# A second level of the fast product for 40 instead of 18 products of a fused attention and feed-forward kernel, with a new order of its instructions

## The chip, the cores and the metric

One Trainium2 chip, one of its cores. The metric is device time in microseconds (us) of one execution; three runs of the kernel before took 904.32, 905.68 and 908.74, median 905.68. Engines: TensorE (PE in the profile, PEld for its weight loads), VectorE (DVE), ScalarE (ACT), GpSimd (POOL), and SyncE (SP), which here only issues DMAs.

## The reference

Attention over keys and values that are averaged in groups of 8 rows, and a feed-forward layer on its output:

```python
batch, n_heads, seq, head_dim = (8, 8, 576, 64)
k_p = k.reshape(B, H, Sp, pool, D).mean(axis=3)      # pool = 8, Sp = 72
v_p = v.reshape(B, H, Sp, pool, D).mean(axis=3)
scores = scale * np.matmul(q, k_p.transpose(0, 1, 3, 2))
scores = scores - np.max(scores, axis=-1, keepdims=True)
attn = np.exp(scores)
attn = attn / (np.sum(attn, axis=-1, keepdims=True) + 1e-09)
o = np.matmul(attn, v_p).astype(np.float32)
x = np.ascontiguousarray(o.transpose(0, 2, 1, 3)).reshape(B * S, H * D)   # 4608 x 512
h = x @ w_in                                          # 512 x 2048
s = np.sin(alpha * h)
g = h + s * s / (alpha + 1e-09)
return (g @ w_out).astype(np.float32)                 # 2048 x 512
```

All in float32.

## The kernel before

*Units and groups.* The 4608 tokens are cut into nine units of 512 (u = 0 to 8); the first layer's 2048 columns into four groups (J = 0 to 3), so that one group makes a block of 512 tokens by 2 x 2 x 128 columns. Each group is multiplied by the Winograd form of Strassen's scheme: tokens, contraction and columns are each halved, and seven products M1 to M7 replace eight. The sums of weight blocks are made once (`combine_w_in`, L671), those of the activations once per unit (`sums_of_x`, L796, four sums on VectorE into the tile `home3`, called `bt`). A product is four matmuls of 128x128 weights by 256 tokens (L834), added in place in PSUM: M1 is copied to where M6 is added (L810), that sum to where M7 is added, M5 is copied to SBUF (`p5`); M2, M3 and M4 complete the four quarters, with sums on VectorE (L809).

*The second level.* For units 1 to 6 some products are themselves done by seven products of half size (`inner_product`, L1002): M5 in groups 2 and 3, M1 in group 3, three per unit and 18 in all. Each is seven matmuls of 128 columns (L1014) in four steps: `a` (two products into a scratch bank, copied by ScalarE at L1018 and L1020), `b` (two, then the copy of L1024), `d` (one, then VectorE's sum of L1029) and `e` (two). Its weights are made once on GpSimd (`inner_w_in`, L769), its eight sums of activations once per unit (`inner_x`, L782, GpSimd, L794), at slot 2 of the unit that uses them.

*After the products,* for each of the four quarters: ScalarE takes the sine (L984) and the scaled square (L991), VectorE adds (L1036), and the block `h` goes to DRAM (`store_g`, L1047). There are two `h` buffers, and one tile `s` for all sines.

*Attention, alongside.* During unit u, batch u + 1's attention is worked in: `two_scores` (L294, matmuls of L308), maxima and differences on VectorE (L331, L332), exponentials on ScalarE (L357, with a table load before and after), sums and reciprocals on VectorE (L363, L364), scaling on GpSimd (L365), 32x32 turns on VectorE (L491 and after), and 16 DMAs that move the turned weights into `aM` (`move`, L504). `all_values` (L590; matmuls of L600 and L613) multiplies by the values, and `to_x` (L513) copies the result out of PSUM into the next activations (L527). `turn_q` (L206) turns a later batch's queries; `k_t` transposes pooled keys, and L270 copies them. Loads of q, k and v and their pooling on GpSimd (L127) come in between.

*What sets the order.* The order on each engine is the order in which the program issues instructions. `hidden` (L806) goes through 28 slots per unit, seven per group: in each it issues group work, and at one fixed place (`extras`) the attention's pieces, which `carry` (L1154) has entered under slot numbers. PSUM has eight banks: five rotate among the groups' four accumulators and attention (`bank`, L747), and banks 5 to 7 serve scores, values and the second level. After the nine units, the second layer (`outputs`, L1262) runs the same scheme twice over, as matmuls of 128x144 (L1312).

Of the kernel before, what the change touches and what calls it, by code (L numbers as in the profile page):

```python
# [36 lines left out]

class Kernel:
# [91 lines left out]
    def load_v(self, b):  # L133
# [13 lines left out]
        self.pool_rows(t, vm[:])  # L147
# [58 lines left out]
    def turn_q(self, b, part):  # L206
# [5 lines left out]
        if part == 0:  # L212
            self.tr = self.new_tr()
        tr = self.tr[:, 0:2560].rearrange("p (k x) -> p k x", k=2)
        if part == 0:
            for e in range(2):
                x = main[:, 4 * e:4 * e + 4].rearrange("p hp t (k i) -> p hp t k i", i=32).rearrange("p hp t k i -> p (hp t) k i")
                out = tr[:, :, 768 * e:768 * e + 512].rearrange("p k (n i) -> p n k i", i=32)
                nc.vector.transpose(out=out, in_=x)
                if e == 0:  # L220
                    self.finish_before()
            return
# [15 lines left out]

    def new_tr(self):
        return self.ap.tile([P, 20 * 5 * 32], F32, name="tr")[:]  # L240
# [8 lines left out]
    def attention(self, b):  # L249
# [14 lines left out]
        def k_t():  # L264
            kp = self.kp.pop(b)
            m = Sp // 3
            ps = self.abank([P, 3, NP * m])
            for j in range(3):
                nc.tensor.transpose(ps[:, j, :], kp[:, j].rearrange("p e d -> p (e d)"), self.ident[:NP * m, :NP * m])
            nc.vector.tensor_copy(out=kb[:].rearrange("p hp (x j) -> p j hp x", j=3), in_=ps.rearrange("p j (hp x) -> p j hp x", hp=NP))  # L270
# [23 lines left out]
        def two_scores(j):  # L294

            x = (self.turn + 1) % 5
# [14 lines left out]
            two_shifts()  # L311
            if j == 0:
                two_shifts()
# [53 lines left out]
        def new_a():  # L367
            self.aM = self.ap.tile([P, 4, 736], F32, name="aM")
# [86 lines left out]
        def a0_views():  # L455

            x = self.aM[:].rearrange("p a x -> p (a x)")[:, 0:5 * S].rearrange("p (h n) -> p h n", h=5)
            return x[:, 0:4], x[:, 4]
# [26 lines left out]
        def turn(i):  # L485
            if i == 0:
                self.tr = self.new_tr()
# [16 lines left out]
        def move(blocks, queue=nc.sync, halves=(0, 1)):  # L504

            tr = self.tr[:, 0:2944].rearrange("p (c s x) -> p c s x", c=2, s=2)
            for a in blocks:
                for s in halves:
                    for c in range(2):
                        r, w = 64 * s + 32 * c, 704 if c else 736  # L510
                        queue.dma_start(out=self.aM[r:r + 32, a, 0:w], in_=tr[32 * a:32 * a + 32, c, s, 0:w])
# [18 lines left out]
        def value_parts(hp, rest):  # L530
# [9 lines left out]
            if rest:  # L540
                r = 64 * s
                at = lambda r, n, i: self.aM[r:r + n, 2 * g:2 * g + 2, 640 + 32 * i:672 + 32 * i]
# [3 lines left out]
            at = lambda r, n, h: order(self.aM[r:r + n, :, 128 * h:128 * h + 128])  # L546
# [3 lines left out]
        def values(hps, banks, n, d):  # L550
# [8 lines left out]
            if d == 0:  # L559
                self.bt[0] = self.home(3, [P, 4, 2, TH])  # L560
            turned = [o.rearrange("p (t j) -> p j t", t=4) for o in ps]

            def differences():
                for kk, o in enumerate(turned):
                    y = self.bt[0][:, 0, kk] if d else self.xT[0][:, kk, 0:TH]
                    f = lambda x: x.rearrange("p (j t) -> p j t", t=4)
                    nc.vector.scalar_tensor_tensor(out=f(self.bt[0][:, d, kk]), in0=o[:, TH // 4:TH // 2, :], scalar=1.0 / POOL, in1=f(y),
# [22 lines left out]
        def all_values():  # L590

            hps = 0, 2, 1, 3
            ps = dict(zip(hps, (self.psum([P, 4 * P], i) for i in (5, 6, 7, (self.turn + 4) % 5))))
            rest = self.psum([P, 4, 64], (self.turn + 1) % 5)
# [20 lines left out]
            self.behind_order()  # L615
            self.behind_order = lambda: None
            for hp in hps:
                to_x(ps[hp].rearrange("p (t j) -> p j t", t=4), hp, 0, 512)
            to_x(rest, slice(0, 4), 512, 64)

        return SimpleNamespace(**{f.__name__: f for f in (k_t, q_t, products, score, two_scores, two_shifts, exp, norm, new_a, turn, move, values, values_rest, all_values,
# [125 lines left out]
    def bank(self, shape, i=None):  # L747

        if i is None:
            i = self.turn = (self.turn + 1) % 5  # L750
        return self.psum(shape, i)
# [17 lines left out]
    def inner_w_in(self):  # L769

        w = self.q_tile(0)[:]
        at = 0
        for p, J0 in ((5, 2), (1, 3)):
            n = self.NJ - J0
            A = self.A[p][:].rearrange("p k (J j m) -> p k J j m", j=2, m=P)[:, :, J0:]
            L = lambda i, j: A[:, j, :, i]
            s1, s2, s3, s4 = (w[:, at + i * n * P:at + (i + 1) * n * P].rearrange("p (J m) -> p J m", m=P) for i in range(4))
            at += 4 * n * P
            self.sums(((s1, L(1, 0), L(1, 1), OP.add), (s2, s1, L(0, 0), OP.subtract), (s3, L(0, 0), L(1, 0), OP.subtract), (s4, L(0, 1), s2, OP.subtract)))
            self.W2[p] = J0, {1: L(0, 0), 2: L(0, 1), 3: s4, 4: L(1, 1), 5: s1, 6: s2, 7: s3}  # L780

    def inner_x(self, u):  # L782

        for p, x, out in ((5, self.bt[u][:, 0], self.last[:, 0:4 * P]),
                          (1, self.xT[u][:, 0:2, 0:TH], self.ex[:, 5].rearrange("p h x -> p (h x)")[:, 0:4 * P])):
            R = lambda i, j: x[:, i, j * P:(j + 1) * P]
            t1, t2, t3, t4 = (out[:, i * P:(i + 1) * P] for i in range(4))
            self.sums(((t1, R(0, 1), R(0, 0), OP.subtract), (t2, R(1, 1), t1, OP.subtract), (t3, R(1, 1), R(0, 1), OP.subtract), (t4, R(1, 0), t2, OP.subtract)))
            self.X2[p] = {1: R(0, 0), 2: R(1, 0), 3: R(1, 1), 4: t4, 5: t1, 6: t2, 7: t3}

# [5 lines left out]
    def sums_of_x(self, u, n):  # L796

        nc = self.nc
        if u not in self.bt:
            self.bt[u] = self.home(3, [P, 4, 2, TH])  # L800
        xT, bt = self.xT[u], self.bt[u]
# [4 lines left out]
    def hidden(self, u, extra):  # L806

        nc = self.nc
        add = lambda o, x, y: nc.vector.tensor_tensor(out=o, in0=x, in1=y, op=OP.add)  # L809
        copy = lambda o, x: nc.scalar.copy(out=o, in_=x)  # L810
        sin, square, early = self.sin, self.square, lambda G: G.J == (0 if G.u else 1)
        two = 0 < u < self.B - 1

        def begin(J):

            b1, b6, b5, b7 = (self.bank([P, JW, TH]) for _ in range(4))
            new = lambda n, **kw: self.hp.tile([P, 2, JW, 2, TH], F32, name=n, **kw)
            G = SimpleNamespace(u=u, J=J, b1=b1, b5=b5, b6=b6, b7=b7, g=new("h"), s=self.s,
                                p5=None, i1=None, i5=None, early=J == (0 if u else 1))
            if two and J > 1:  # L820
                G.i5 = self.inner_product(G, 5, b5, 7)
            if two and J == 3:
                G.i1 = self.inner_product(G, 1, b1, 6)
            return G

        def product(G, p, ps, start=False, part=range(4)):

            xT, bt = self.xT[G.u], self.bt[G.u]
            B = lambda i, j: xT[:, 2 * i:2 * i + 2, j * TH:(j + 1) * TH]
            x = {1: B(0, 0), 2: B(1, 0), 3: B(1, 1), 4: bt[:, 3], 5: bt[:, 0], 6: bt[:, 1], 7: bt[:, 2]}[p]  # L830
            for n in part:
                jj, kk = divmod(n, 2)
                f = G.J * JW + jj
                nc.tensor.matmul(ps[:, jj, :], self.A[p][:, kk, f * P:(f + 1) * P], x[:, kk, :],  # L834
                                 start=(start and n == 0), stop=(kk == 1), skip_group_check=True)

        def squares(Q, i):

            if i == 0 and not Q.early:
                square(Q, 0, 1)  # L840
            if i == 1:
                square(Q, 1, slice(0, 2))

        self.squares = squares
        for slot in range(7 * self.NJ):
            J, k = divmod(slot, 7)
# [396 lines left out]

# [329 lines left out]
```

## Time and profile before

The profiled execution lasted 902.6 us from first to last instruction.

| stretch, us | what | TensorE busy |
|---|---|---|
| 0 to 20 | loads, batch 0 | 17.22 |
| 20 to 77 | unit 0 | 56.78 |
| 77 to 132.6 | unit 1, turned into unit 2 | 55.62 |
| 132.6 to 408.0 | the turns to unit 7, five units of 55.0 to 55.1 | all |
| 408 to 510 | units 7 and 8, no attention | all |
| 537 to 902 | second layer | 361.05 |
| runs of the kernel | 904.32 to 908.74, median 905.68 | |
| profiled execution | span 902.6 | 895.0 |

TensorE's granted clock was 1.00 in every stretch. One matmul in float32 shows as two rows of L834, L1014 or L1312. A line of the timeline gives start, length, engine, line, what it writes and reads, the shape, and how many were merged; a bracket gives the engine's idle time before it and what ended that.

### The profile page before, as it was taken

To read this page: it belongs to the slowest core of one execution; us is meant where nothing else is said; L and a number is where in the kernel's file an instruction comes from. 1 tells how busy PE (TensorE), PEld (TensorE's weight loads), DVE (VectorE), ACT (ScalarE), POOL (GpSimd) and SP (SyncE) were. 2 spreads that over 40 slices of the span, in tenths; PEclk is the share of its full clock that TensorE was granted. 3 is DMA by queue.
4 is the path that set the end of the run, shared out by engine and by line. 5 is a ranking of instruction groups with operands and counts; after the bars stand their busy time and mean duration, and the time that the engine had idled before them with its cause. 6 is when DMAs were issued, how large, how long until landed. Compare 5 with 4: busy or idle time off the path is not lost.

```text
span 902.6 us, 17941 instructions
## 1 busy us (share of the span) xinstructions
PE 895.0 (99%) x7014; PEld 815.8 (90%) x7014; DVE 677.4 (75%) x1011; ACT 448.3 (50%) x1070; POOL 210.5 (23%) x216
## 2 busy tenths in 40 slices
PE   8999999999999999999999999999999999999998
PEld 5787888888888888888888999999999999999997
DVE  7685766768577685764458799979798888889895
ACT  5696776877768778687976611111111111111111
POOL 4788552824438253430000000000000000000000
PEclk9999999999999999999999999999999999999999
DMA  9965867759586595648216346261618162534401
GB/s 261 245 200 158 220 163 202 196 167 251 139 213 186 177 230 143 176 146 293 93 72 227 102 141 199 59 194 38 224 27 230 33 197 67 172 92 127 137 15 40
DMA packets 128747, 141.13 MB, mean 156 GB/s; under 512 B 46920, under 2 KB 95704, under 8 KB 128664
## 3 DMA queue, kind: packets, MB, share of 16 engines
q1 hardware_dynamic: 125880, 137.88, 53.2%
q10 hardware_dynamic: 2784, 2.11, 0.9%
q8 instruction: 56, 0.92, 0.4%
q14 instruction: 27, 0.22, 0.1%
HBM read 75.37 MB, written 47.19 MB: 136 GB/s over the span
## 4 chain that ended last, share of the span: by engine, by line
PE 91%; DMA 3%; DVE 2%; POOL 2%; SPq 1%; issue 0%; ACT 0%; DVEq 0%; POOLq 0%
PE PS L834 42%; PE PS L1312 41%; PE PS L1014 3%; PE PS L308 2%; PE PS L600 2%; DMA a<-in_moe_w_in_dram 2%; DMA kvin<-in_v_dram 1%; SPq L669 1%; PE PS L613 1%; DVE x L1267 1%; DMA h<-in_k_dram 1%; POOL kvin L131 0%; POOL as L675 0%; DVE s L1267 0%; POOL ex L365 0%
## 5 line engine op out<-in xcount | busy, mean ns | idle before, releaser
L834 PE MATMUL PS<-home,a 128*128 128x256 f32 x1104 | 257.9, 381 | 0.7 <-ACT home L527 0.5
L834 PEld LDWEIGHTS PS<-home,a 128*128 128x128 f32 x1104 | 205.2, 190 | 34.1 <-issue 5.0
L834 PE MATMUL PS<-home,as 128*128 128x256 f32 x768 | 183.0, 382 | 0.0
L834 PEld LDWEIGHTS PS<-home,as 128*128 128x128 f32 x768 | 141.6, 190 | 19.8 <-ACT PS L810 1.2
L1312 PE MATMUL PS<-s,wb 128*128 128x144 f32 x896 | 119.1, 286 | 0.0
L1362 POOL TENSOR_TENSOR cc<-cc,cb 128x576 f32<-128x576 f32 x1 | 2.0, 1976 | 501.8 <-DVE cb L1267 501.8
L1312 PEld LDWEIGHTS PS<-s,wb 128*128 128x128 f32 x896 | 113.7, 190 | 0.1
L991 ACT ACTIVATE s<-s,c 128x256 f32<-128x256 f32 (+1 forms) x228 | 113.5, 564 | 0.0
L809 DVE TENSOR_TENSOR h<-PS,p 128x512 f32<-128x512 f32 x72 | 49.2, 683 | 64.2 <-PE PS L834 36.3
L131 POOL TENSOR_TENSOR kvin<-kvin 96x768 f32<-96x768 f32 (+3 forms) x42 | 71.6, 1705 | 69.5 <-DMA kvin<-in_v_dram 67.9
L1440 ACT COPY PS<-PS 128x144 f32<-128x144 f32 x56 | 14.7, 263 | 145.0 <-PE PS L1312 135.5
L984 ACT ACTIVATE s<-h,al 128x256 f32<-128x256 f32 x144 | 65.6, 510 | 39.4 <-DVE h L809 39.3
L1312 PE MATMUL PS<-r,wb 128*128 128x144 f32 x512 | 73.3, 286 | 0.3 <-DVE r L1267 0.3
L1312 PE MATMUL PS<-s,a 128*128 128x144 f32 x512 | 73.2, 286 | 0.0
L1036 DVE TENSOR_TENSOR h<-PS,s 128x512 f32<-128x512 f32 x36 | 24.7, 687 | 59.8 <-ACT s L991 59.8
L984 ACT ACTIVATE s<-PS,al 128x256 f32<-128x256 f32 x144 | 60.1, 470 | 18.6 <-PE PS L834 17.7
L1312 PEld LDWEIGHTS PS<-r,wb 128*128 128x128 f32 x512 | 67.1, 190 | 0.5 <-DVE r L1267 0.5
L1312 PEld LDWEIGHTS PS<-s,a 128*128 128x128 f32 x512 | 67.1, 190 | 0.0
L810 ACT COPY PS<-PS 128x512 f32<-128x512 f32 x72 | 41.5, 576 | 35.0 <-PE PS L834 30.4
L1460 ACT COPY PS<-PS 128x144 f32<-128x144 f32 x56 | 14.7, 263 | 88.1 <-PE PS L1312 88.1
L1312 PE MATMUL PS<-s,we 128*128 128x144 f32 x384 | 54.9, 286 | 0.0
L1312 PE MATMUL PS<-x,wb 128*128 128x144 f32 x384 | 54.9, 286 | 0.0
(215 smaller groups left out, 1407.7 us busy)
## 6 DMA issues: line engine op xcount, KB each, us to landing
g_bridge<-h SPq DMA_DIRECT2D x72, 512.0 KB
r<-g_bridge SPq DMA_DIRECT2D x31, 1152.0 KB
out_dram<-o SPq DMA_DIRECT2D x122, 72.0 KB
kvin<-in_k_dram SPq DMA_DIRECT2D x14, 576.0 KB
q<-in_q_dram SPq DMA_DIRECT2D x7, 1024.0 KB
kvin<-in_v_dram SPq DMA_DIRECT2D x14, 512.0 KB
aM<-tr SPq DMA_DIRECT2D x54, 92.0 KB
aM<-tr SPq DMA_DIRECT2D x54, 88.0 KB
```

The source lines that it names most:

```text
L131: self.nc.gpsimd.tensor_tensor(out=t[..., 0:w] if w > D else out, in0=t[..., 0:w], in1=t[..., w:2 * w], op=OP.add)
L308: nc.tensor.matmul(ps[e][r0 + r:r0 + r + q.shape[-1], h, :], q[s], kb[s, hp, :], start=True, stop=True)
L600: nc.tensor.matmul(o[r:r + 64], w, x, start=start and i < 2, stop=False, skip_group_check=True)
L809: add = lambda o, x, y: nc.vector.tensor_tensor(out=o, in0=x, in1=y, op=OP.add)
L810: copy = lambda o, x: nc.scalar.copy(out=o, in_=x)
L834: nc.tensor.matmul(ps[:, jj, :], self.A[p][:, kk, f * P:(f + 1) * P], x[:, kk, :], start=(start and n == 0), stop=(kk == 1), skip_group_ch ...
L984: self.nc.scalar.activation(out=G.s[:, i, jj, j, :], in_=src[:, jj], func=AF.Sin, scale=self.al[:, f:f + 1])
L991: self.nc.scalar.activation(out=x, in_=x, func=AF.Square, scale=self.c[:, f:f + 1])
L1014: nc.tensor.matmul(o, W[m][:, G.J - J0], X[m], start=start and n == 0, stop=True, skip_group_check=True)
L1036: add = lambda o, x, y: self.nc.vector.tensor_tensor(out=o, in0=x, in1=y, op=OP.add)
L1312: nc.tensor.matmul(out, W[:, J // 2, J % 2, :], A[:, J, :], start=(start and J == 0), stop=(J == self.NJ - 1), skip_group_check=True)
L1440: nc.scalar.copy(out=x1[:, 0, :], in_=x0[:, 1, :])
```

## The change

1. The second level is used for M5 in groups 0, 2 and 3 and M1 in all four groups, of units 1 to 6, except group 0 of unit 1: 40 products. Where a group has both, they go side by side: each step issues both products' matmuls, and one instruction copies or adds for both.
2. Banks are fixed: M5 in 0, M1 in 1, M6 in 2, M7 in 3 and 4 by turns; the scratch of the second level is bank 7, and scores and values use the one left over and 5 to 7.
3. The turned attention weights are moved by DMA into the memory of the exponentials (`ex`) instead of `aM`; two memsets clear unused rows (`clean`) and one writes the constant column again (`mark`). `aM` then holds second-level weights.
4. Slots become an agenda: each piece of work has a number, all are sorted by it and issued in that order. Group work is listed in quarters of a product (`M3.2` is the third matmul of M3) and single copies, by kind of group; attention pieces (`"U"`) likewise. `inner_x` for the next unit, made in slot 2 of that unit before, is issued right after the values, and the next unit's first second-level step (`i.a`) before the unit begins.

```diff
+INNER = {5: (0, 2, 3), 1: (0, 1, 2, 3)}
+ORDER = {
+"U": {
+    "load_v": -0.6771, "load_k0": -0.67645, "scores0": 2.23415, "shift0": 2.7041, "shift1": 2.76275, "scores1": 6.3989, "shift2": 6.51235,
+    "shift3": 8.54465, "exp0": 8.7107, "exp1": 8.8037, "exp2": 8.80775, "exp3": 8.8134, "pool_vm": 9.29605, "norm1": 9.842, "norm2": 9.84325,
+    "norm0": 9.85195, "pool_k0": 9.86815, "pool_v": 9.88775, "turn1": 12.0494, "turn2": 12.0874, "norm3": 12.1291, "load_q": 13.2604, "turn3": 14.4892,
+    "turn0": 14.5697, "move": 18.6305, "load_k1": 18.6308, "qa": 20.6435, "clean": 24.1271, "values": 24.1272, "qb": 24.1272, "pool_k1": 24.1273,
+    "out0": 24.1273, "out3": 24.1274, "mark": 24.1274, "out2": 24.1275, "sx0": 24.1276, "inner_x": 24.1276, "out4": 24.8897, "k_t": 25.4917, "k_c": 25.9324,
+    "qc": 26.1053, "out1": 26.453, "sx1": 27.2068, "qd": 27.3209, "qe": 27.3222, "sx2": 30.3883, "sx3": 30.7192},
...
+"mid0": {
+    "i.a": -1.94585, "i.ca": -1.2117, "i.b": -0.2106, "i.cb": 0.1784, "i.cm": 0.4379, "i.d": 1.56985, "i.ad": 1.6811, "i.e5": 1.8197, "p5": 2.0064,
+    "i.e1": 2.07495, "c16": 2.17285, "M6.0": 3.207, "M6.1": 3.5662, "M2.0": 3.70575, "M2.1": 3.961, "M2.2": 4.1451, "M2.3": 4.16925, "M6.2": 4.2005,
+    "M6.3": 4.2101, "c67": 4.92375, "s00": 5.0421, "M3.0": 6.5015, "q00": 6.78125, "M3.1": 7.51875, "a00": 8.5183, "M3.2": 8.75365, "M7.0": 8.7555,
+    "M3.3": 8.7571, "M7.1": 8.8054, "M7.2": 8.8184, "M7.3": 8.8661, "a01": 8.8673, "a11": 9.17105, "M4.0": 9.5295, "s01": 9.6997, "M4.1": 11.0128,
+    "M4.2": 11.0459, "q01": 11.964, "s11": 11.9667, "M4.3": 12.1709, "s10": 12.1969, "q1": 12.1984, "f1": 12.3193, "f10": 14.2497, "st": 15.1528},
...
+"mid3": {
+    "i.a": -4.5662, "i.ca": -2.6829, "i.b": -2.68275, "i.cb": -2.6827, "i.cm": -2.53285, "i.d": -2.49785, "i.ad": -2.3645, "i.e1": -1.9251, "i.e5": -1.8136,
+    "c16": -0.7185, "M6.0": -0.3243, "M6.1": -0.2635, "M6.2": 0.0164, "M6.3": 0.2375, "p5": 0.6291, "M2.0": 0.8793, "c67": 1.2237, "M2.1": 1.24255,
+    "M7.0": 3.14685, "M2.2": 3.2053, "M2.3": 3.21935, "M7.1": 3.23455, "s00": 3.9005, "M7.2": 4.34775, "M7.3": 4.64365, "M3.0": 4.78415, "q00": 5.10045,
+    "a11": 5.12815, "a00": 5.1486, "M4.0": 5.6839, "M3.1": 6.28755, "M4.1": 7.33955, "M3.2": 7.82165, "s11": 8.0521, "M3.3": 8.64085, "M4.2": 8.75265,
+    "a01": 8.9832, "M4.3": 9.0252, "s01": 9.2725, "s10": 9.3563, "q1": 11.5988, "q01": 15.8032, "f1": 16.5407, "f10": 16.8426, "st": 19.1772},
+}
...
         def new_a():
-            self.aM = self.ap.tile([P, 4, 736], F32, name="aM")
+            self.aM = self.ap.tile([P, 4, 736], F32, name="aM")[:].rearrange("p a x -> p (a x)")
+            self.aT = self.ex[:, 0:5].rearrange("p i h x -> p (i h x)")[:, 0:2944].rearrange("p (a x) -> p a x", a=4)
+
+        def clean():
+            for r in (32, 96):
+                nc.gpsimd.memset(self.aT[r:r + 32, :, 704:736], 0.0)
+
+        def mark():
+            nc.gpsimd.memset(ex[:, 0:5, :, Sp:Sp + 1], 1e-9)
...
-                        queue.dma_start(out=self.aM[r:r + 32, a, 0:w], in_=tr[32 * a:32 * a + 32, c, s, 0:w])
+                        queue.dma_start(out=self.aT[r:r + 32, a, 0:w], in_=tr[32 * a:32 * a + 32, c, s, 0:w])
...
-            for hp in hps:
-                to_x(ps[hp].rearrange("p (t j) -> p j t", t=4), hp, 0, 512)
-            to_x(rest, slice(0, 4), 512, 64)
+            self.outs = [lambda hp=hp: to_x(ps[hp].rearrange("p (t j) -> p j t", t=4), hp, 0, 512) for hp in hps]
+            self.outs.append(lambda: to_x(rest, slice(0, 4), 512, 64))
...
+        acts = {
+            "p5": p5,
+            "c16": lambda: copy(G.b6[:], G.b1[:]),
+            "c67": lambda: copy(G.b7[:], G.b6[:]),
+            "s00": lambda: self.sin(G, 0, 0, G.b1),
...
+            "q1": lambda: self.square(G, 1, slice(0, 2)),
...
+            "a11": lambda: add(g()[:, 1, :, 1], G.b7[:], G.p5[:]),
+            "a01": lambda: add(g()[:, 0, :, 1], G.b6[:], G.p5[:]),
+            "a00": lambda: add(g()[:, 0, :, 0], G.b1[:], G.s[:, 0, :, 0]),
+            "f10": lambda: add(g()[:, 1, :, 0], G.b7[:], G.s[:, 1, :, 0]),
+            "f1": lambda: add(g()[:, :, :, 1], g()[:, :, :, 1], G.s[:, :, :, 1]),
+            "st": lambda: self.store_g(G),
+        }
+        for p in range(1, 8):
+            for i in range(4):
+                acts[f"M{p}.{i}"] = lambda p=p, i=i: product(p, i)
+        for x in ("a", "ca", "cm", "b", "cb", "d", "ad", *(f"e{p}" for p in G.l2)):
+            acts[f"i.{x}"] = lambda x=x: G.i[x]()
+        where = ORDER[self.kind(n)]
+        for m, f in acts.items():
+            if m in where:
+                self.at(7 * n + where[m], f)
+
+    def banks(self, n):
+        if n < self.NJ:
+            return {p: (2 + 4 * n + i) % 5 for i, p in enumerate((1, 6, 5, 7), 1)}
+        return {5: 0, 1: 1, 6: 2, 7: 4 - n % 2}
...
+    def at(self, key, f, *a):
+        self.agenda.append((key, len(self.agenda), (lambda: f(*a)) if a else f))
+
+    def perform(self, until):
+
+        self.agenda.sort(key=lambda x: x[:2])
+        while self.agenda and self.agenda[0][0] < until:
+            self.agenda.pop(0)[2]()
...
+        def a():
+            for j, m in enumerate((1, 5)):
+                for i, p in enumerate(ps):
+                    product(p, m, y[:, i, j], i == j == 0)
+
+        def ca():
+            nc.scalar.copy(out=f[:, :, 0], in_=y[:, :, 0:1].to_broadcast([P, k, 2, P]))
+
+        def cm():
+            m5.append(self.sm.tile([P, 2, 1, P], F32, name="m5", bufs=1)[:, 0:k])
+            nc.scalar.copy(out=m5[0], in_=y[:, :, 1:2])
+
+        def cb():
+            nc.scalar.copy(out=f[:, :, 1, 0], in_=f[:, :, 0, 1])
+
+        def ad():
+            nc.vector.tensor_tensor(out=f[:, :, :, 1], in0=x[:, :, P:3 * P].rearrange("p k (i t) -> p k i t", i=2), in1=m5[0].to_broadcast([P, k, 2, P]), op=OP.add)
+
+        acts = {"a": a, "ca": ca, "cm": cm, "b": lambda: products((6, 1), (2, 0)), "cb": cb, "d": lambda: products((7, 2)), "ad": ad}
+        for i, p in enumerate(ps):
+            acts[f"e{p}"] = lambda i=i, p=p: [product(p, m, f[:, i, c // 2, c % 2]) for m, c in ((3, 1), (4, 2))]
+        return acts
```

In the tables a group's numbers count from its own first slot (seven slots a group), those of `"U"` from its unit's; `i.…` are the second level's steps, `qa` to `qe` the turns and moves of queries, `outN` the values' copies-out, `sxN` the sums of `bt`.

## The prediction

> **What bounds the kernel now.** First the head of the page, its engine shares and the chain that ended last:
>
> ```profile
> span 902.6 us, 17941 instructions
> PE 895.0 (99%) x7014; PEld 815.8 (90%) x7014; DVE 677.4 (75%) x1011; ACT 448.3 (50%) x1070; POOL 210.5 (23%) x216
> PE 91%; DMA 3%; DVE 2%; POOL 2%; SPq 1%; issue 0%; ACT 0%; DVEq 0%; POOLq 0%
> ```
>
> TensorE (PE) is the end's path almost alone, so only two things can change the time much: how many TensorE rows there are, and how long TensorE stands between them. Busy shares overstate, since matmuls are pipelined; so I next read TensorE's instructions in order of time, in the fourth of the units that repeat, and take the pitch from one start to the next:
>
> ```profile
> 228.61 2.75 PE L834 MATMUL PS<-home,a 128*128 128x256 f32 x12
> 231.20 0.38 PE L1014 MATMUL PS<-home,q 128*128 128x128 f32 x2
> 231.42 0.39 PE L1014 MATMUL PS<-last,as 128*128 128x128 f32 x2
> 231.65 1.03 PE L834 MATMUL PS<-home,a 128*128 128x256 f32 x4
> ```
>
> A matmul shows as two rows. Twelve rows of 256 columns take 2.59 us (228.61 to 231.20): 0.216 us a row. Four rows of 128 columns take 0.45 (231.20 to 231.65); over the unit's pairs I read 0.1115 a row. Then the turn of a unit, where a batch's values are multiplied, and one busy stretch of ScalarE (ACT):
>
> ```profile
> 187.62 0.65 PE L600 MATMUL PS<-aM,vm 64*64 64x512 f32 x6
> ...
> 189.96 1.14 PE L613 MATMUL PS<-aM,vz 32*128 32x512 f32 x8
> 191.03 1.99 PE L834 MATMUL PS<-home,a 128*128 128x256 f32 x8
> 191.12 2.61 ACT L527 ACTIVATE home<-PS 128x320 f32<-128x320 f32 x9 [1.35 <-PE PS L613]
> ...
> 193.73 0.55 DVE L270 COPY kblk<-PS 128x288 f32<-128x288 f32 x1
> ```
>
> ```profile
> 221.86 0.84 ACT L984 ACTIVATE s<-PS,al 128x256 f32<-128x256 f32 x2
> 222.59 0.90 ACT L991 ACTIVATE s<-s,c 128x256 f32<-128x256 f32 x2
> 223.38 0.90 ACT L984 ACTIVATE s<-h,al 128x256 f32<-128x256 f32 x2
> 224.19 0.37 ACT L1018 COPY PS<-PS 128x256 f32<-128x256 f32 x1
> ```
>
> The values take 3.41 us of TensorE; ScalarE copies them out only 0.09 after their last row has gone in, in nine pieces over 2.6 us. Back to back, a pair of sines from PSUM costs ScalarE 0.73, a pair of squares 0.79.
>
> One whole unit, from values to values (132.62 to 187.69):
>
> ```profile
> 132.62:187.69 55.07, 55.07 (x450) 47.22 (x453) 38.41 (x64) 41.17 (x96) 25.56 (x25) 1.00 0.71 192
> ```
>
> (TensorE, weight loads, VectorE, ScalarE, GpSimd, then the granted clock.) Summed by pitch, that unit holds 200 rows of 256 (43.16), 42 rows of 128 (4.68), scores (1.26 + 1.47), values 3.41 and the keys' transposes 0.25: 54.23. So 0.83 us of the 55.06 is TensorE standing: some 0.15 to 0.2 at each score block, 0.1 before the values, under 0.1 behind copies. Six such units: 5.0 us. Units 7 and 8 run 448 rows in 96.89 us, 0.216 each: nothing stands there, and I read no gap worth counting in unit 0 after its first loads, nor in the second layer, which keeps its instructions.
>
> **The change, part by part.**
>
> *Products.* 22 more first-layer products go from 8 rows of 256 (8 x 0.2158 = 1.726) to 14 rows of 128 (14 x 0.1115 = 1.561): 0.165 each, **-3.6 us**. A full unit then needs 168 x 0.2158 + 98 x 0.1115 + 2.73 + 3.41 + 0.25 = 53.57.
>
> *Work on the other engines.* Two products side by side share three ScalarE copies (0.576 for 512 columns, as L810; 0.375 for 256, as L1018, twice: 1.33) and one VectorE sum over 512 columns (0.68, as L809). A unit goes from three single products (2.70 on ScalarE, 1.30 on VectorE) to three pairs and one single (4.88 and 2.48); one group's squares become two instructions of 512 in place of four of 256 (-0.6). ScalarE goes from 41.2 to 42.7 us a unit, VectorE from 38.4 to 39.6, GpSimd (POOL) from 25.6 to 26.3 with three more memsets: none is the bound by its total. It matters where they stand.
>
> *Banks and order.* All the old stalls (5.0) may go with the new order; what takes their place has to be worked out at the waits. I set T = 0 when the values' last row is in, and add rows.
>
> The turn of a unit, new order. TensorE: seven quarter products (0.43 each) and the keys' transposes 0.25: 3.3; then the next unit's first pair begins (i.a, eight rows of 128, to 4.2), two quarters of the group before (M4.0, M3.1), and i.b at 5.0. ScalarE: four copies-out from 0.1 to 2.1, the group's sines to 2.8 and squares to 3.7; the last copy-out; then i.b's copy (0.58), which needs VectorE's a00. VectorE: the sum sx0 from 1.9 to 2.6, the key copy to 3.1, a turn of queries (0.66, spacing 0.6) to 3.7, a11 to 4.4, a00 to 5.0. So M4.0 waits for a11 until 4.5 and i.b for the copy until 5.0 + 0.05 + 0.58 + 0.1 = 5.7: **0.7 us per turn, five turns, 3.3 us**. Behind the waiting a00 stands VectorE's next sum, and i.b is followed by i.d, which needs it.
>
> Inside the unit I set each wait against the rows between: the wait costs its operation plus 0.2 from the last row to the start (225.29 to 225.49 for a copy) plus 0.1 back. First pair, ad (0.68 + 0.3) against two quarters (0.86): 0.12. Second group, i.b behind the exponentials' table load (1.28) and first exponential: 0.12. Third and fourth groups: VectorE has f1 (1.17 to 1.93 in the rows of L1036) just ahead of ad, 0 to 0.5 each; I take 0.15, since f1 may start early. Together 0.54, times six: **3.1 us**, between 1.0 and 6.
>
> *The eight small sums* (inner_x) were 20 us ahead of their first use; now they begin after sx0 and the pair's second rows want the first two at once:
>
> ```profile
> L794 POOL TENSOR_TENSOR last<-home x12: 455/903/962, 87.4 to 364.7; 128x128 f32<-128x128 f32 x12
> L794 POOL TENSOR_TENSOR last<-home,last x12: 447/782/902, 88.0 to 365.6; 128x128 f32<-128x128 f32 x12
> ```
>
> Minimum, median, maximum in ns. All eight took 5.86 us at 142.50, 0.73 each. From 2.65 that gives pairs of sums at 4.1, 5.6, 7.0, 8.5, against uses at 3.7, 5.7, 7.6 and 8.9: covered but for 0.4 that the wait for a11 hides. At 0.45 each nothing is late; at 0.9 each i.b waits 0.6 more per turn (3 us). I take the middle, nothing.
>
> [...]
>
> *Turned weights in the exponentials' memory.* The sixteen moves (L511) are the same in number and bytes; `clean` and `mark` are small memsets (0.45 for the two of L1158) off the path. If mark were late, the small sums queued behind it on GpSimd would be.
>
> *Slots and stores.* The store of the fourth group (`st`) now stands just ahead of a00 of the second group after it, which takes the same buffer: a new DMA wait on VectorE. Its f10 ends some 5.5 us before that a00 is wanted, and a lone store issued at 182.58 had its traffic done by 186.9, 4.3 us. Covered by about 1 us; each us beyond that costs six. SP's queue holds the loads of values and keys ahead of it, issued 20 us earlier.
>
> *Weights* for the second level are now made for all columns: about 5 us more GpSimd work around 80 to 90 us, whose first use lies near 99. Nothing.
>
> Sum: -3.6 (rows) - 5.0 (old standing) + 3.3 + 3.1 = **-2.2 us** on the span of 902.6. The runs' median is 905.68, 3.1 above that span; I carry it along: **903.4**. That is 0.25% less, inside the 0.5% (4.5 us) that a measurement of this kernel tells from no change.
>
> **The rivals.**
>
> *The order closes nearly all gaps.* For: TensorE's pieces are now placed in quarters, and the covers I found short are short by 0.1 to 0.2. Against: the chain through one bank (first copy to a00) grows to about 11 of the group's 13.5 us. With 0.4 us of standing per unit: -3.6 - 5.0 + 2.5, **899.6**. Chance 0.32.
>
> *The turn becomes a real wait on the small sums (slower).* If sx0 waits for all five copies-out (4.3, not 1.9 on) and the sums take 0.9, the fourth is ready near 8 and i.b stands 2 us more at each of five turns: **912**. It makes the kernel slower from 1.4 us per turn beyond my sum. For: the medians above, and six operations in a row on three engines there. Against: GpSimd is otherwise empty then. Chance 0.18.
>
> *The rows are not cheaper.* If in runs of eight a row of 128 cost what 144 columns cost in the second layer (360.9 / 2944 = 0.1226), a product would gain 0.01 and nothing is saved: **907**. Against: 0.112 in the four rows above. Chance 0.05.
>
> My forecast has 0.45; with the last rival 0.50 for within 0.5%, 0.32 faster, 0.18 slower. The forecast's own range is 901 to 906; for 8 in 10 it reaches to both neighbours, 898 to 910.5.
>
> **What would show it.** 98 rows of 128 per unit at 0.111; a unit of 54.6 us or so; i.b standing 0.5 to 1 after the values; ad just behind f1 in the third group. A unit under 54.0 means the covers hold; over 55.5, that the turn or the store decides. I am wrong if unit 7, 8 or 0 lose time, or if VectorE waits for the store.

## The result and the profile after

The changed kernel takes **946.02 us** (median of four runs, 943.26 to 947.5), the one before 905.06 (904.32 to 908.74) beside it: ratio 1.0441 [1.0414, 1.0467], 41 us slower. The forecast was 903.4 with a range up to 910.5. Its profiled execution lasted 945.5 us. The page's head: span, engines' busy time with share and count, the chain that ended last by engine.

```profile
span 945.5 us, 18309 instructions
PE 911.3 (96%) x7146; PEld 814.4 (86%) x7146; DVE 676.7 (72%) x1016; ACT 454.6 (48%) x1073; POOL 207.0 (22%) x235
...
PE 59%; SPq 13%; DMA 10%; POOL 9%; DVE 3%; issue 3%; ACT 3%; POOLq 0%; DVEq 0%; ACTq 0%
```

The chain was TensorE's by 91% before; now a third of it is SP's queue, DMA and GpSimd. No engine has become the bound: VectorE, ScalarE and GpSimd are as busy as before, in a longer span. From values to values (the start of the last value rows) the six repeating intervals take 53.53, 55.06, 55.07, 55.25, 55.06, 55.07 before (so not all of the five units were 55.0 to 55.1) and 53.91, 61.28, 62.30, 61.88, 65.14, 62.61 after: 38.1 of the 42.9 us between the two spans. Unit 0 adds 5.0; all that follows the last values takes as long as before.

Lines of the changed kernel in what follows: L929 and L1019 are the matmuls of 256 and of 128 columns, L699 and L712 those of the values, L404 the scores, L362 the keys' transposes (`k_t`) and L366 their copy (`k_c`), L317 and L320 the turns of queries (`qa` to `qe`), L590 and L593 those of the attention weights, L458 the scaling by the norms, L231 the pooling. L1032, L1036, L1039 and L1042 are a pair's `i.ca`, `i.cm`, `i.cb` and `i.ad` ("ad" below), L909 a group's sums on VectorE (a00, f1 and so on), L910 its copies, L997 and L1004 its sines and squares.

One unit, from values to values (length, then TensorE, weight loads, VectorE, ScalarE, GpSimd, granted clock, DMA share, GB/s):

```profile
201.55:263.85 62.30, 58.39 (x472) 48.31 (x470) 38.56 (x65) 42.75 (x96) 23.08 (x28) 0.97 0.61 170
```

Its 98 rows of 128 columns cost what I took. TensorE's own lines at the turn (start, length, with the wait in the bracket):

```profile
205.68 0.47 PE L362 MATMUL PS<-ident,kp 96*128 96x96 f32 x3 [0.64 <-POOL kp L231]
...
209.30 0.46 PE L1019 MATMUL PS<-last,q 128*128 128x128 f32 x2 [0.24 <-ACT PS L1032]
209.59 0.39 PE L1019 MATMUL PS<-ex,aM 128*128 128x128 f32 x2
209.82 0.39 PE L1019 MATMUL PS<-home,as 128*128 128x128 f32 x2
210.04 0.39 PE L1019 MATMUL PS<-home,a 128*128 128x128 f32 x2
```

Two rows in 0.22 us, 0.112 each. At i.b, where I looked for the loss, TensorE stands 0.24; ahead of the keys' transposes, where I put nothing, it stands 0.64. The small sums were the slower rival's mechanism; on GpSimd they run at 0.41 us spacing, eight of them between 205.66 and 209.03 (first and last shown, with VectorE's sum of two SBUF tiles that began beside the last ones):

```profile
205.66 0.46 POOL L891 TENSOR_TENSOR last<-home 128x128 f32<-128x128 f32 x1
...
208.57 0.46 POOL L891 TENSOR_TENSOR ex<-home,ex 128x128 f32<-128x128 f32 x1
```

```profile
208.40 1.17 DVE L899 TENSOR_TENSOR home<-home,home 128x512 f32<-128x512 f32 x1
```

Here it was VectorE's that took longer (1.17 for what takes 0.69 in the median of this line), and at three more of the five turns (1.10 each); at the last turn VectorE's took 0.67 and the small sum at 396.71, where the turn's other seven take 0.45 to 0.47, 1.16. In e6 below, one small sum took 0.90 beside VectorE's 0.72. In the changed kernel that is 0.41 to 0.70 us a turn.

Most of the time is in a place that I didn't look at. SP's queue, first before, then after (start, time to issue them all, line, what is moved, how many). The values' last rows go in at 191.03 before and 202.62 after.

```profile
188.69 10.35 SPq L234 DMA_DIRECT2D q<-tr  x16
199.13 5.54 SPq L1050 DMA_DIRECT2D g_bridge<-h  x4
204.76 1.53 SPq L140 DMA_DIRECT2D kvin<-in_v_dram  x2
...
218.88 2.04 SPq L121 DMA_DIRECT2D kvin<-in_k_dram  x2
227.47 10.60 SPq L511 DMA_DIRECT2D aM<-tr  x16
```

```profile
207.32 11.17 SPq L330 DMA_DIRECT2D q<-tr  x16
218.54 1.12 SPq L1052 DMA_DIRECT2D g_bridge<-h  x2
219.70 2.20 SPq L240 DMA_DIRECT2D kvin<-in_v_dram  x2
...
248.87 10.10 SPq L610 DMA_DIRECT2D ex<-tr  x16
259.02 0.58 SPq L221 DMA_DIRECT2D kvin<-in_k_dram  x1
```

These issues stand in program order, and sixteen moves take 10.1 to 11.2 us, 0.63 to 0.70 apiece, in which SP issues nothing else. Before, the query moves began 2.3 us *ahead* of the values' end; now they begin 4.7 *behind* it, since `qc` stands on VectorE behind the keys' copy `k_c`, which needs `k_t`, which needs `pool_k1`, which needs `load_k1`, which SP issues only behind the weight moves. The links, at the turn above (`load_k1` had left at 196.71, behind sixteen weight moves):

```profile
201.74 2.90 POOL L231 TENSOR_TENSOR kvin<-kvin 96x768 f32<-96x768 f32 x2 [16.24 <-DMA kvin<-in_k_dram]
```

```profile
206.19 0.56 DVE L366 COPY kblk<-PS 128x288 f32<-128x288 f32 x1 [1.00 <-PE PS L362]
206.62 0.68 DVE L320 STREAM_TRANSPOSE tr<-q 64x512 f32<-64x512 f32 x1
```

Behind the query moves the third group's store leaves at 218.54, the values' load at 219.70 (17.1 us from the values' end, 13.7 before), the norms begin at 32 (28), the weight moves at 46 (36), and `load_k1` leaves at 259.02, 56 us after the values, where before both halves left at 28. On it the next turn's `k_t` waits, and so the next query moves: a closed ring. Who waits, on VectorE, then on the weight loads and on TensorE's rows (total us, times, longest):

```profile
DVE h L909 <- DMA g_bridge<-h: 9.2, 4, 2.6
```

```profile
PEld PS L1019 <- ACT PS L1032: 16.8, 16, 2.6
PE PS L1019 <- ACT PS L1032: 12.8, 15, 2.2
PE PS L362 <- POOL kp L231: 3.8, 4, 1.4
PE PS L699 <- DMA ex<-tr: 2.8, 3, 1.3
```

All four waits of a00 (the sum that empties M1's bank into an `h` buffer) are for the third group's store, the one right behind the query moves; the fourth group's, whose cover I had worked out, holds nothing here. A late a00 holds the copy L1032, which writes into the same bank, and that the pair's rows. The store is the smaller part of the 12.8: after its four waits TensorE's rows stand 3.4 us. Five other stands for L1032, 7.8 us, come from the late load of the values: GpSimd's pooling and scaling start late, and VectorE's turns of weights wait for them with the second group's a00 behind. In one unit:

```profile
230.41 3.71 POOL L231 TENSOR_TENSOR kvin<-kvin 128x1024 f32<-128x1024 f32 x2 [21.39 <-DMA kvin<-in_v_dram]
```

```profile
236.07 0.71 DVE L590 STREAM_TRANSPOSE tr<-ex 128x512 f32<-128x512 f32 x1 [3.36 <-POOL ex L458]
```

The a00 behind it begins at 239.24, L1032 at 239.96 and the pair's rows, after a stand of 1.98, at 240.59.

### The profile page after: what moved, and what is told of

Its sections match the earlier page's. It is cut to its first block, busy times and chain, and to the rows that moved or that the text cites. A ratio compares the mean times of both kernels' runs of the same rounds, so it can differ in the third digit from the quotient of the medians.

```text
span 945.5 us, 18309 instructions
## 1 busy us (share of the span) xinstructions
PE 911.3 (96%) x7146; PEld 814.4 (86%) x7146; DVE 676.7 (72%) x1016; ACT 454.6 (48%) x1073; POOL 207.0 (22%) x235
## 4 chain that ended last, share of the span: by engine, by line
PE 59%; SPq 13%; DMA 10%; POOL 9%; DVE 3%; issue 3%; ACT 3%; POOLq 0%; DVEq 0%; ACTq 0%
PE PS L1305 40%; PE PS L929 16%; SPq L330 5%; SPq L610 5%; POOL kvin L231 4%; DMA kvin<-in_v_dram 4%; POOL ex L458 2%; DMA q<-in_q_dram 2%; DMA kvin<-in_k_dram 2%; POOL vr L231 1%; DVE h L909 1%; DMA a<-in_moe_w_in_dram 1%; PE PS L699 1%; PE PS L1019 1%; ACT s L997 1%
## 5 line engine op out<-in xcount | busy, mean ns | idle before, releaser
L929 PE MATMUL PS<-home,a 128*128 128x256 f32 x968 | 246.7, 383 | 0.7 <-DVE h L909 0.4
L929 PEld LDWEIGHTS PS<-home,a 128*128 128x128 f32 x968 | 177.5, 191 | 31.3 <-issue 4.7
L929 PE MATMUL PS<-home,as 128*128 128x256 f32 x728 | 191.6, 383 | 1.5 <-ACT PS L910 1.2
L929 PEld LDWEIGHTS PS<-home,as 128*128 128x128 f32 x728 | 133.1, 190 | 21.4 <-ACT PS L910 1.3
L1004 ACT ACTIVATE s<-s,c 128x256 f32<-128x256 f32 (+1 forms) x216 | 113.3, 582 | 0.3 <-ACT s L997 0.3
L231 POOL TENSOR_TENSOR kvin<-kvin 96x768 f32<-96x768 f32 (+3 forms) x42 | 68.9, 1641 | 197.3 <-DMA kvin<-in_v_dram 111.8
L909 DVE TENSOR_TENSOR h<-PS,s 128x512 f32<-128x512 f32 x72 | 48.6, 679 | 66.4 <-ACT s L1004 55.1
L997 ACT ACTIVATE s<-h,al 128x256 f32<-128x256 f32 x144 | 64.5, 503 | 18.0 <-DVE h L909 17.9
L997 ACT ACTIVATE s<-PS,al 128x256 f32<-128x256 f32 x144 | 60.4, 476 | 10.8 <-PE PS L929 10.7
L910 ACT COPY PS<-PS 128x512 f32<-128x512 f32 x72 | 41.5, 576 | 46.3 <-PE PS L929 23.1
L909 DVE TENSOR_TENSOR h<-h,s 128x1024 f32<-128x1024 f32 x36 | 46.1, 1280 | 18.7 <-ACT s L1004 18.5
```

The source lines that it names most:

```text
L231: self.nc.gpsimd.tensor_tensor(out=t[..., 0:w] if w > D else out, in0=t[..., 0:w], in1=t[..., w:2 * w], op=OP.add)
L997: self.nc.scalar.activation(out=G.s[:, i, jj, j, :], in_=src[:, jj], func=AF.Sin, scale=self.al[:, f:f + 1])
L1004: self.nc.scalar.activation(out=x, in_=x, func=AF.Square, scale=self.c[:, f:f + 1])
```

## The experiments

"Unit" is the mean of the second to fifth interval from values to values (55.11 before, 62.65 after); the store's wait is that of VectorE's sums into `h`, in all.

| kernel | median us | ratio to before, 95% | unit | store's wait |
|---|---|---|---|---|
| after | 946.02 | 1.0414 to 1.0467 | 62.65 | 9.2 |
| e1 | 954.08 | 1.0510 to 1.0567 | 64.23 | 26.5 |
| e2 | 941.11 | 1.0373 to 1.0417 | 61.48 | 11.7 |
| e3 | 932.26 | 1.0262 to 1.0377 | 59.44 | 10.0 |
| e4 | 932.46 | 1.0276 to 1.0328 | 58.88 | 15.3 |
| e5 | 922.32 | 1.0155 to 1.0195 | 57.41 | 0.6 |
| e6 | 916.95 | 1.0091 to 1.0138 | 56.10 | 0.6 |
| e7 | 945.81 | 1.0413 to 1.0459 | 62.40 | 24.5 |
| e8 | 941.58 | 1.0365 to 1.0409 | 60.41 | 24.5 |
| e9 | 917.82 | 1.0124 to 1.0162 | 56.22 | 0 |
| e10 | 916.49 | 1.0104 to 1.0134 | 55.84 | 0.8 |
| e11 | 915.10 | 1.0098 to 1.0128 | 56.08 | 0 |
| b1 | 922.47 | 1.0172 to 1.0206 | 58.57 | 0 |
| e12 | 917.38 | 1.0113 to 1.0157 | 56.24 | 0.5 |
| e13 | 931.20 | 1.0255 to 1.0299 | 58.97 | 0 |
| e14 | 931.24 | 1.0267 to 1.0310 | 58.92 | 0 |
| e15 | 926.36 | 1.0220 to 1.0248 | 58.25 | 0 |

### Which load closes the ring? (e1 to e4)

First I took a load for the cause, the keys' (theory K) or the values' (V), or else the pairs' own chain (P).

```diff
-"load_k1": 18.6308
+"load_k1": 9.3
```

> Edit: the second load of keys is issued just after the first pooling of values (number 9.3) and so ahead of the 16 moves of turned weights on SP's queue, not behind them. Theory V (the ring closes through the load of values, which stands behind the 16 moves of queries): the load of keys only ran beside the path over the values, about 1 us shorter, so a unit falls from 62.3 to about 61 and the time from 946 to 938 to 942. Theory K (the ring closes through this load: moves 10.1 us, load 5.2, pooling 3.9, then keys' transposes): about 8 us a unit, down to the 55 of before, 905 to 910. Theory P (the second level's own waits through one bank set the unit): no change, 944 to 948.

Slower than after, and outside all three ranges. On SP, `load_k1` needs a buffer that `pool_vm` frees, so the two halves hold the queue from 224.75 for 10.26 us, and the fourth group's store behind them leaves at 235.06: a00 waits 3.35 us for it, until 242.37.

```diff
-"load_v": -0.6771, "load_k0": -0.67645
+"load_v": -0.6801, "load_k0": -0.68
```

> Edit: the loads of values and of the first keys are issued just ahead of the moves of queries on SP's queue (numbers -0.6801 and -0.68, 27.3199 in the unit's own count, where the moves have 27.3209), nothing else. Theory V: the values land some 11 us sooner in the unit, the pooling, scaling and turning of weights follow, and the unit falls to TensorE's own time with short waits: 54.5 to 55.5, total 901 to 908. Theory K: the load of keys behind the weights' moves still closes the ring, 935 to 944. Theory P: 944 to 948.

Five us less, in theory K's range, which e1 had spoken against: the values' load now leaves at 195.62, but the query moves behind both loads end at 218.5 all the same.

> Edit: both of the first two. Theory V: as the second run or 1 to 3 us below it, 900 to 906, since the pooling of keys then no longer ends late ahead of the keys' transposes. Theory K: 903 to 908, and the first run has nearly all of it. Theory P: 944 to 948.

(e1 and e2 together.) 932, better than either and no theory's number, with a third of the loss gone. What was left: scores waiting for `q<-tr` and stores held behind the moves. So neither load is the ring by itself.

```diff
 (e3, and)
-"qc": 26.1053
+"qc": 26.15
```

> Edit: both load edits, and VectorE's turn of the remaining queries (qc) goes behind a11 and a00 at the turn of a unit, not ahead of them. If the wait of 0.7 us per turn that the prediction worked out (a11 and a00 late by that turn's 0.6) is real, five turns give back 0.4 to 0.6 each, 2 to 3 us below the third run. If the copies out or the sums on GpSimd come last there, no change (within 0.7 us).

No gain: with `qc` later the weight loads of the scores wait 6.3 us for the moves, 3.2 in e3. That points at the moves themselves.

### The query moves (e5, and b1 in the kernel before)

```diff
-"qc": 26.1053, "qd": 27.3209, "qe": 27.3222
+"qc": 24.12721, "qd": 24.12722, "qe": 24.12723
```

> Only the query's last turns and their sixteen moves go early: qc, qd and qe stand right behind qb, ahead of the values' results and of the keys' copy on VectorE, as before; the loads of values and keys keep the slots of the change. Theory Q (the late query moves push everything behind them on SP's queue: the stores, load_v, and with these the norms and the weight moves, by about 7 us): the moves end by about 2 us after the next unit's start, load_v lands some 7 us earlier, the ring of 62.2 us falls to 56 or 57 a unit, and the whole to 915 to 925. Theory L (the places of load_v and load_k1 decide, and the moves only fill time in which the queue waits): units of 61 to 62, 935 to 946. Theory P (the second level's own waits through one bank): no change, 946.

922: the three numbers, with no load touched, take 24 of the 41 us away. The queue of e5 (the values' last rows go in at 196):

```profile
194.87 11.00 SPq L330 DMA_DIRECT2D q<-tr  x16
205.97 1.07 SPq L1052 DMA_DIRECT2D g_bridge<-h  x2
207.08 2.26 SPq L240 DMA_DIRECT2D kvin<-in_v_dram  x2
...
237.37 10.09 SPq L610 DMA_DIRECT2D ex<-tr  x16
247.50 0.58 SPq L221 DMA_DIRECT2D kvin<-in_k_dram  x1
```

The moves begin a microsecond ahead of the values' end again, and the store and the load behind them leave 10 and 11 us after it. The store's wait falls from 9.2 to 0.6 and the weight loads' wait for L1032 from 16.8 to 1.9. Theory L, for which the loads' places decide, asked for 935 or more.

The converse, in the kernel before, with its products, banks and loads:

```diff
-at(((turn, turn + 1) if u == 0 else (23, 24))[part] if part < 2 else turn + part, self.turn_q, u + 2, part)
+at(turn + part if u == 0 else (23, 27, 27, 27)[part], self.turn_q, u + 2, part)
```

> The kernel before with one thing of the change alone: the last query turns and their sixteen moves go behind the values' results and the keys' copy (slot 27 of the unit for 24 to 25). Theory Q (the place of these moves on SP's queue makes the ring, whatever the products and banks are): the moves begin some 7 us later, the stores, load_v and the weight moves with them, and it is 12 to 35 us slower, 918 to 940. Rival (the ring needs the change's other slots, the keys' load behind the weight moves above all; the queue before has slack enough): under 910.

17 us slower, from one place of the change alone: 

```profile
200.59 10.88 SPq L234 DMA_DIRECT2D q<-tr  x16
211.57 1.07 SPq L1050 DMA_DIRECT2D g_bridge<-h  x2
212.74 2.23 SPq L140 DMA_DIRECT2D kvin<-in_v_dram  x2
```

The moves begin 6 us behind the values' end (194.6), the values' load 18. Both directions agree, so the moves' place is shown as the main cause. Its price shows in other waits here: no sum waits for a store; TensorE's rows stand 7.2 us at the scores for `q<-tr` and 4.0 for the copy L810. Both edits also move the turns of queries on VectorE; that the queue, and not these, carries the price is read from the waits, since no run moved the one without the other.

### The rest of the ring (e6, e10)

```diff
 (e5, and)
-"load_k1": 18.6308
+"load_k1": 13.27
```

> e5 with load_k1 put right behind load_q (13.27 for 18.63), so that it isn't behind the sixteen weight moves. Theory Q: what is left of the ring goes through load_k1, POOL's pool_k1 and the keys' transposes; it takes 1 to 2 us a unit off e5, 910 to 918. Theory L: this is one of the two that decide, so it takes 3 us a unit or more off e5. Theory P: 946.

5.4 us less, in theory Q's range; theory L asked for 3 us a unit or more. The wait of L362's weight loads for the pooled keys (8.6 us in e5) is gone.

```diff
 (e6, and)
-"pool_k0": 9.86815
+"pool_k0": 12.2
```

> e6 with the first half of the keys' pooling (pool_k0, 3.5 us on GpSimd) moved from ahead of the last norm to behind it (slot 12.2 for 9.87), as before. In e6 the weight moves begin 40.1 us after the values' end, in the kernel before 36.4, with the same place of the values' load within 4 us. Theory Q (what is left of the late ring is this pooling): the weight moves begin 3.5 us earlier, the waits for them at the values (2 us in the first unit, 0.7 in the fifth) go, 912 to 915. Rival (the rest is all standing inside the units and the first unit): 916 to 918.

The first interval says yes (53.75 instead of 56.43); the median, on the rival's number, can't be told from e6. What was gained came back elsewhere. TensorE's rows no longer wait for the weight moves at the values (2.6 us in e6), but the pooling now runs on GpSimd from 284.01 to 287.77, beside the first group's last sum f1, which takes 1.77 where it took 1.25 in e6, and the third group's pair waits for ad behind it:

```profile
285.15 1.77 DVE L909 TENSOR_TENSOR h<-h,s 128x1024 f32<-128x1024 f32 x1 [0.20 <-ACT s L1004]
```

```profile
287.58 0.49 PE L1019 MATMUL PS<-home,aM 128*128 128x128 f32 x2 [0.47 <-DVE PS L1042]
```

By the distances of the starts that pair stands 0.63 here and 3.2 in all six units, against 1.1 in e6. The ring no longer decides; one unit of e10:

```profile
249.81:305.81 56.00, 55.53 (x474) 46.56 (x470) 38.24 (x65) 42.56 (x96) 24.33 (x28) 1.00 0.67 189
```

### The store (e7, e8, e12)

```diff
 (e6, and)
-"load_v": -0.6771
+"load_v": -3.85
```

> e6 with load_v right behind the query moves (slot 24.15 in place of 27.32), as early as its buffer allows. Theory Q: load_v was already early in e6, so within 3 us of e6, and units near 55. Theory L: another 2 us a unit, 12 us in all. Theory P: 946.

Wrong by 29 us (945.81 is theory P's number, but not by its mechanism, as e12 shows), and so again in e8, which has SP's order of the kernel before:

```diff
 (e7, and)
-"load_k0": -0.67645, "pool_k0": 9.86815
+"load_k0": 13.265, "pool_k0": 18.7
```

> SP's queue in the order of the kernel before: query moves early, load_v, load_q, then both halves of the keys together, then the weight moves; pool_k0 goes behind the norms on POOL. Theory Q: close to e7, 900 to 912. Theory L: the same 900 to 912, and then e5 alone shows which it was. Theory P: 940 or more.

The queue of e7 shows why, and VectorE's waits:

```profile
203.63 10.30 SPq L330 DMA_DIRECT2D q<-tr  x16
213.98 1.36 SPq L240 DMA_DIRECT2D kvin<-in_v_dram  x2
215.38 2.69 SPq L245 DMA_DIRECT2D vr<-in_v_dram  x4
218.17 1.93 SPq L1052 DMA_DIRECT2D g_bridge<-h  x2
```

```profile
228.32 0.69 DVE L909 TENSOR_TENSOR h<-PS,s 128x512 f32<-128x512 f32 x1 [5.88 <-DMA g_bridge<-h]
```

The third group's store stands behind six loads, leaves 4 us after the moves and lands in the middle of their traffic, at 228.3; a00 needs its buffer. The new order leaves this store hardly anything to spare. The test:

```diff
 (e10, and)
-"load_v": -0.6771     "mid2" "st": 13.3227
+"load_v": -3.85       "mid2" "st": 10.14
```

> e10 with load_v right behind the query moves, as in e7, but with the third group's store put ahead of it (10.14 in place of 13.32 of that group), where in e7 it stood behind six more loads. Theory S (e7 lost its 29 us through this store alone: it left SP 4 us after the moves and landed 9.6 us later among the values' traffic, and the sum a00 that takes its buffer waited): the wait for the store goes and the time is that of e10 within 3 us, 912 to 918. Rival (the early load of values is bad by itself, by its traffic or by the buffer of the keys): 930 to 945 as e7.

917: the store's place was all of it in e7, and an earlier load of the values is worth nothing. That e8 has the same cause is read from the same wait of 24.5 us only.

### What the 22 products are worth (e9, e11)

```diff
-INNER = {5: (0, 2, 3), 1: (0, 1, 2, 3)}
+INNER = {5: (2, 3), 1: (3,)}
...
+        for p in INNER:
+            if p not in G.l2 and f"i.e{p}" in where:
+                where.update({f"M{p}.{i}": where[f"i.e{p}"] for i in range(4)})
```

> e6 with only the 18 second-level products of the kernel before, in the new order and banks: where a product isn't of the second level its four quarters of 256 columns stand where the pair's last rows stood. Theory R (rows: each of the 22 products is worth 0.165 us and its pair's chain of copies and sums costs nothing more): 3.6 us slower than e6, 920.5. Theory P (the pairs' waits for ScalarE and VectorE, 1.9 us of standing a unit in e6 against 0.8 before, cost more than the rows give): faster than e6 by 1 to 4 us, 913 to 916.

> e10 and e9 together: the loads' order mended, pool_k0 behind the norms, 18 products. Theory R: 3.6 above e10. Theory P: 1 to 4 below e10, 909 to 913. Neither theory expects it below the kernel before, since the first unit keeps its 3 us.

Neither theory's number: e9 lies 0.9 us above e6 and e11 1.4 below e10, with ranges that overlap both times. The rows are cheaper, as counted. But summed from the distances of the matmuls' starts, less 0.2158 or 0.1115 for the row between, TensorE stands 13.0 us over the six intervals of e10 and 10.7 in e11: 2.3 more, against 3.6 from the rows. So in these two traces the 22 products are ahead by 0.7 us over the six intervals (335.6 us against 336.3); in the medians e11 is ahead by 1.4. Their worth can't be told from nothing. (The kernel before stands 5.1 by the same sum; I had 5.0.)

### The sums inside the units (e13 to e15)

```diff
 (e10, and)
-"mid0" "f1": 12.3193   "mid1" "f1": 11.517
+"mid0" "f1": 12.34     "mid1" "f1": 11.64
```

> e10 with the last sum f1 (1.2 us on VectorE) of the first and second group moved from just ahead of the next pair's sum ad to just behind it. In e10 TensorE stands 2.0 to 2.4 us a unit, 0.6 to 0.9 of it before the pair's last rows of the fourth group and some 0.2 before those of the third, both waiting for ad. Theory P (these waits are the part of the pairs' price that I sized too small): 0.7 us a unit goes, 2 to 5 us in all, 911 to 914. Rival (ad is late through what runs ahead of f1, or the sums behind f1 are then late in its place): 915 to 918.

> e12 and e13 together, the best order that these runs point to. If both theories hold: 909 to 914, still above the kernel before, since the first unit keeps 3 us and the units 1 to 1.5 us of standing more than before for 0.66 us of rows.

(e14 is e12 and e13 together.) 15 us slower than e10, both times, where theory P had 2 to 5 less. The expectation of e13 had also taken the two pairs for each other: in e10 it is the third group's that stands 0.15 to 1.08 a unit, the fourth group's stands 0.15.

```diff
 (e10, and)
-"mid1" "f1": 11.517
+"mid1" "f1": 11.64
```

> e10 with only the second group's sum f1 put behind the fourth group's ad. In e13 it was the first group's f1 that did the harm: in e10 it runs from 285.15 while VectorE waits for ScalarE's copy ahead of ad (286.84), in e13 from 295.45 behind ad, and a00 behind it comes that much later. Theory P (ad of the fourth group costs TensorE 0.6 to 0.9 us a unit, since f1 runs ahead of it): 2 to 5 us less than e10, 911 to 914. Rival (here too what stands behind f1 is late in its place): 916 or more.

10 us slower with one sum moved by one place. VectorE and ScalarE in e15:

```profile
304.79 0.70 DVE L1042 TENSOR_TENSOR PS<-PS,m 128x512 f32<-128x512 f32 x1 [0.24 <-PE PS L1019]
305.39 1.22 DVE L909 TENSOR_TENSOR h<-h,s 128x1024 f32<-128x1024 f32 x1
```

```profile
306.64 1.70 ACT L997 ACTIVATE s<-h,al 128x256 f32<-128x256 f32 x4 [2.52 <-DVE h L909]
308.25 0.57 ACT L910 COPY PS<-PS 128x512 f32<-128x512 f32 x1
```

f1 is no mere filler: it reads the one tile `s`, into which the next group's sines go. They wait for it on ScalarE until 306.61, and the copy queued behind them (L910 at 308.25) releases TensorE's next rows, which stand 1.75 us for it. Ahead of the fourth group's ad f1 costs 0.15 a unit; behind it a unit takes 2.4 us more (58.25 against 55.84), most of it this stand (for L910 TensorE's rows stand 8.7 us over the six intervals here, 15.1 in e13, and nothing that the profile counts in e10).

## Why the prediction was wrong, by its steps

*Slots and stores* is the step that failed, with a term that *The turn of a unit* put at nothing. The step worked out the cover of one store, the fourth group's ("Covered by about 1 us"), and of SP's queue it says that it "holds the loads of values and keys ahead of it, issued 20 us earlier". The loads leave 5 to 10 us ahead of that store, and the cover held. But the queue's order wasn't gone through: the turn had counted `qc` as 0.66 us of VectorE, and that sixteen DMAs leave behind it was costed nowhere. They had begun 2.3 us ahead of the values' end and now began 4.7 behind, with the third group's store, the values' load and, a round later, `load_k1` behind them. e5 gives the price of their place in the changed kernel, 24 of 41 us, and b1 in the old one, 17.

The second omission is in the same step: `load_k1` behind the weight moves closes a ring through `pool_k1`, the keys' transposes and `k_c` (5.4 us, e6).

*Products*, -3.6: right; 0.112 and 0.216 a row, 176 rows of 256 fewer and 308 of 128 more.

*Old standing*, -5.0: the size was right (5.1), but it was taken to go whole without a reason. In e10 1.1 us at the scores and 0.6 ahead of the values are still there.

*The turn*, 3.3 (five of 0.7 are 3.5): the sum is right by luck. In e10 the six turns stand 3.1, in pieces of 0.04 to 0.17; i.b, on which I put the 0.7, stands 0.09 to 0.17 and 0.07 within its rows. *Inside the unit*, 3.1: too small; 8.2 in e10. With the scores and the values that is 13.0 of standing where the sum had 6.4. The largest piece is the third group's ad, 0.54 a unit in the mean where I took 0.15; in e6, without the pooling beside f1, it was 0.18. I had noted that f1 stood ahead of ad and not that it must.

*The eight small sums*: nothing, as taken. In the changed kernel they do end late (209.03, the pair's rows at 209.30) because `pool_k1` runs ahead of them on GpSimd, again the ring. The slower rival (its five turns of 2 us more make 913, not 912) named the wrong mechanism, though the right side.

*Unit 0*, of which the prediction said that it would be wrong if it lost time: 5.0 us longer after, 3.1 in e10. In the changed kernel 2.8 of the 5.0 lie ahead of its first row, 1.9 of them one wait for a load of queries; in e10 0.9. From its first row on TensorE idles 2.0 us in e10 against 0.2 before, 1.2 of it for copies on ScalarE (L910). No run tried to mend this. Its other sign, a wait of VectorE for a store, came too (9.2 us).

So e10, the change with its order mended, stands 9.9 us of span above the kernel before (11.4 in the medians): 3.1 in unit 0 and 6.6 in the six units (8 us more standing, 2 us of rows saved there, the rest not assigned). No version here beats the kernel before.

## What to carry to other kernels

A piece of work that is moved takes its DMA issues along: list what each queue issues, in order, before and after, and follow a late one round until it comes back to itself. Here sixteen small moves were 10.1 to 11.2 us in which nothing else left that queue, so they belong where the queue would stand idle, and stores whose buffers are wanted soon belong ahead of them. And a sum that frees a single buffer is work for the engine that waits for the buffer, whatever it costs its own.

## What the runs showed of the hardware

*Half clock after some stands.* In the changed kernel TensorE stood 1.98 us for L1032 and then ran at half clock (window, TensorE, weight loads, VectorE, ScalarE, GpSimd, clock, DMA share, GB/s; below it TensorE's rows):

```profile
238.00:240.00 2.00, 0.61 (x3) 0.19 (x1) 1.97 (x5) 0.04 (x1) 2.00 (x2) 1.00 0.23 62
240.00:241.00 1.00, 0.41 (x2) 0.42 (x3) 1.00 (x2) 1.00 (x3) 0.92 (x2) 0.87 0.02 5
241.00:242.00 1.00, 1.00 (x7) 1.00 (x6) 0.12 (x1) 1.00 (x2) 0.92 (x3) 0.50 0.06 16
...
244.00:245.00 1.00, 1.00 (x8) 0.89 (x7) 0.20 (x1) 0.47 (x2) 0.92 (x3) 0.93 0.54 207
```

```profile
240.59 0.69 PE L1019 MATMUL PS<-last,q 128*128 128x128 f32 x2 [1.98 <-ACT PS L1032]
241.07 0.64 PE L1019 MATMUL PS<-ex,aM 128*128 128x128 f32 x2
241.50 0.63 PE L1019 MATMUL PS<-home,as 128*128 128x128 f32 x2
```

The rows' spacing doubles to 0.43 for two. The half-clock stretches in the units of all these runs last 3.41 or 6.83 us. All twelve stands from 3.28 to 5.58 us in the units came with one (e1, e7 and e8). Of those between 1.59 and 2.22, three did (1.98 here, 2.03 in e6, 2.07 in e7) and 25 did not (the five of 1.75 in e15, 2.16 in the changed kernel, 2.22 in e4 among them); in e3 two stands of 0.77 and 0.46 us within 4 us brought one, in the changed kernel one of 1.33 with one of 0.23 behind it. So the wait of 1.98 us here cost up to 1.7 more (half of 3.41), and each of the twelve from 3.28 us on up to 1.7 or 3.4: in e1 these stretches add up to 23.9 us, in e7 to 20.5, at most half of which is lost, so up to 10 of e7's 29 us are the clock's and not the wait's own. What sets a stretch off was not shown: stands of 1.59 to 2.22 us came with one and without.
